# Query projection of an attention branch as seven half-size products over pairs of token blocks, placed between the first products of a spectral branch

## The chip, the cores and the metric

One core of one Trainium2 chip. The metric is the device time of one execution in microseconds (us). TensorE (PE) multiplies, its weight loads are shown as PEld; VectorE (DVE), ScalarE (ACT) and GpSimd (POOL) work on tiles; SyncE (SP) issues the DMAs.

## The reference

Two independent branches write the two halves of each output row. x is 2048 x 1024 in both, all in float32.

```
# attention with 32 query heads of width 32 and one shared key/value head
q = (x @ wq) in 32 heads;  k = x @ wk;  v = x @ wv          # wq 1024x1024, wk and wv 1024x32
p = softmax(q k^T * 32**-0.5);  a = concat_heads(p v) @ wo  # wo 1024x1024
# spectral branch: real part of a 2-D Fourier transform by given matrices
re = xb @ dft_hid_re.T;  im = xb @ dft_hid_im.T
b = dft_seq_re @ re - dft_seq_im @ im
return concatenate([a, b], -1)
```

## The kernel before

**Products.** A float32 product is made of three matmuls of rounded parts (`hi` times `hi`, `hi` times `lo`, `lo` times `hi`). A `Group` is one 128x512 output in one PSUM bank: its `left` items are weights (128 x 4 x 128 each), its `right` items 128x512 operands, and it has three matmuls for each right operand. One such matmul is a *fill*; `pos["fill"]` counts them. The query projection has 4 token blocks x 8 groups of 128 output columns, each with 8 right operands (24 fills). Keys and values have one group of 24 fills for each block. The spectral branch is two stages of seven half-size products each (a Winograd form of Strassen's method): `STAGE1` with 16 groups of 12 fills for each product p1, p2, p6, p7, p5, p3, p4 in that order, then `PRODUCTS` with groups of 24. Last comes the output projection with groups of 24.

**Attention.** 32 units, one for each token block b and query group g, with 32 steps each. A step makes the scores twice on TensorE: `scores` (tile `pss`) for row maxima on VectorE (`nm`) and row sums on ScalarE, and for an earlier unit `expo` (tile `pst`), transposed, whose exponential on ScalarE is the tile `p`. Every eighth step `pv` multiplies four chunks of `p` with the values. `open_unit` fetches a unit's query (`qh_d`, `ql_d`) from DRAM and needs its stores to have been issued.

**Order.** All groups stand in one list. `take(n)` issues the next n fills; `level` spreads all fills evenly over the 1024 steps and gives none to the step that has a `pv`. The prologue (up to 494 fills) first runs START = 120 fills alone, then 66, then 7 with each of 44 steps that have scores only. `aside` moves a `pv` out of the first and last 6 fills of a group.

**Operands.** `pump` runs after each fill and moves two lines of items forward, `RL` for right operands and `ML` for left ones, each in four stages: load (SyncE), `comb` (sums of up to three terms on GpSimd, in place in `it.t[0]`), `hi` (a rounding cast, ScalarE up to START, then VectorE) and `lo` (the difference, VectorE up to START, then GpSimd). The two lines are

```
RL = Line(NR0, NR, (40, 40, 14, 8), load_r, comb, hi_r, lo)
ML = Line(NM0, NM, (52, 36, 27, 21), load_m, comb, hi_m, lo)
```

with the lead of each stage in fills before an item's due time. `may` lets at most NR0 = NM0 = 3 items be between load and `lo`. A left item is due when its group needs it. The right operands of a new set are due spread over the set before:

```
p0 = prev["set"]
it.due = min(it.need, p0 + (i0 - p0) * (g.first + c + 1) // (len(g.set) * len(g.right)))
```

Every engine and SyncE's queue keep the order in which the program issues.

**Outputs.** `post` of a group moves its PSUM bank to SBUF. For the query it writes `qh` (scaled and rounded) and `ql` (the rest), both on VectorE after START, and stores them. For the spectral stage it copies, or adds to a partial output that was loaded again (`ys`, tile `y`). `store` issues a DMA at once up to START and 9 fills later (`BEHIND`) after that.

The rounded weights of the query are saved in DRAM by block 0 (`wq_d`) and fetched by the other three. The order of the list is: keys and values of blocks 1, 2, 3, 0, the query of blocks 0, 1, 2, 3, the spectral stages, the output projection.

Of the kernel before, what the change touches and what calls it, by code (L numbers as in the profile page):

```python
# [8 lines left out]
F32 = mybir.dt.float32  # L9
F32R = mybir.dt.float32r  # L10
AF = mybir.ActivationFunctionType
ALU = mybir.AluOpType
# [4 lines left out]
P = 128  # L17
# [4 lines left out]
W = 512  # L22
NG = 8
NQ = 4
# [22 lines left out]
STAGE1 = [  # L47
# [7 lines left out]
]  # L55
# [32 lines left out]
def tile_kernel(ctx: ExitStack, tc, xT, wq, wkv, wo, xbT, wT, cT, out):  # L88
    nc = tc.nc
    te = Ordered(tc, nc.tensor)  # L90
    act = Ordered(tc, nc.scalar)
    dve = Ordered(tc, nc.vector)
    gp = Ordered(tc, nc.gpsimd)
    sp = Ordered(tc, nc.sync)
    scale = float(DH) ** -0.5
# [5 lines left out]
    dram = ctx.enter_context(tc.tile_pool(name="dram", bufs=1, space=DRAM))  # L101
# [5 lines left out]
    wq_d = [[[dram.tile([P, 4, P], F32, name=f"wq_{g}_{q}_{a}") for a in range(2)] for q in range(2)] for g in range(NG)]  # L107
# [283 lines left out]
    def x_set(b):  # L391
        return [Item([(lambda c=c: xT[b, c], 1)]) for c in range(ND)]
# [23 lines left out]
    def kv_group(b, xs):  # L416
        return Group(wkv_items, xs, kv_post(b), rows=2 * DH)

    ready = set()
    seen_w = set()  # L420

    def q_group(b, g, xs):
        if g in seen_w:
            left = [Item(None, pre=lambda q=q: wq_d[g][q]) for q in range(2)]
        else:
            seen_w.add(g)
            left = [Item([(lambda q=q: wq[g, :, q * 4:(q + 1) * 4, :], 1)], save=wq_d[g][q]) for q in range(2)]

        def post(ps):
            qh = op.tile([P, W], F32R, name="qh")  # L430
            ql = op.tile([P, W], F32R, name="ql", bufs=1)
            if pos["fill"] <= START:
                act.activation(qh, ps, AF.Copy, scale=scale)
            else:
                dve.tensor_scalar_mul(qh, ps, scale)
            dve.scalar_tensor_tensor(ql, ps, scale, qh.bitcast(F32), op0=ALU.mult, op1=ALU.subtract)
            store(qh_d[b][g], qh)
            store(ql_d[b][g], ql, ("q", b, g))
        return Group(left, xs, post)


    s_d = {(r, e): [dram.tile([P, W], F32, name=f"s{r}{e}_{s}") for s in range(NC)] for r in range(2) for e in range(2)}
    COLS = (((0, 0), (1, 1)), ((1, 0), (0, 1)))

    def stage1():
        for f, (name, lt, rt, outs) in enumerate(STAGE1):
            keeps = any(t[0] == name for p in STAGE1 for t in p[1] + p[2])

            def x_src(t, k):
                if isinstance(t[0], str):  # L450
                    return (lambda: have(("xr", k), xr_d[k]), t[1])
                return (lambda: xbT[t[0] * 8 + k, :, t[1] * 4:t[1] * 4 + 4], t[2])

            def w_src(t, n, c):
                if isinstance(t[0], str):
                    return (lambda: have(("wr", n, c), wr_d[n][c]), t[1])
                r, e = COLS[n][t[0]]
                return (lambda: wT[r, e, t[1] * 4 + c], t[2])

            R = [[Item([w_src(t, n, c) for t in rt], raw=(wr_d[n][c], ("wr", n, c)) if keeps else None) for c in range(4)]  # L460
                 for n in range(2)]
            for k in range(8):
                left = [Item([x_src(t, k) for t in lt], raw=(xr_d[k], ("xr", k)) if keeps else None)]
                for n in range(2):
                    ys, plan = [], []
                    for frm, sg, to in outs:
                        it = None
                        if frm is not None:
                            it = Item([(lambda frm=frm, n=n, k=k: have((n, frm, k), u_d[n, frm][k]), 1)])
                            ys.append(it)  # L470
                        if isinstance(to, str):
                            plan.append((it, sg, u_d[n, to][k], (n, to, k)))
                        else:
                            me, s = COLS[n][to[1]], to[0] * 8 + k
                            plan.append((it, sg, s_d[me][s], (me, s)))

                    def post(ps, plan=plan):
                        for it, sg, to, key in plan:
                            if it is None:
                                o = op.tile([P, W], F32, name="qh")  # L480
                                dve.tensor_copy(o, ps)
                            else:
                                o = it.y
                                (dve.tensor_add if sg > 0 else dve.tensor_sub)(o, o, ps)
                            store(to, o, key)
                    yield Group(left, R[n], post, ys=ys, part=(R, 4 * n))

    hs = {}

    def have(key, ap):  # L490
        assert key in ready, key
        return ap

    def stage2():
        seen, total = {}, {}
# [67 lines left out]

    def x_groups(b, kv, q):
        xs = x_set(b)
        return ([kv_group(b, xs)] if kv else []) + ([q_group(b, g, xs) for g in range(NG)] if q else [])

    first = x_groups(0, True, True)  # L570
    start = x_groups(1, True, False) + x_groups(2, True, False) + x_groups(3, True, False) + first[:2]
# [263 lines left out]
```

## Time and profile before

| | |
|---|---|
| time, median of 3 runs | 2852.16 us (2851.02 to 2853.55) |
| span of the profiled execution, first to last instruction | 2849.5 us |
| product matmuls by the plan | 5664, of which the query projection has 768 |
| mean granted clock of TensorE | 0.998 |
| DMA | 480.83 MB, mean 169 GB/s |

The page gives the span of the profiled execution and not its own time; the median lies 2.7 us above the span. The page's busy shares count the modelled end of each matmul, and matmuls overlap, so the sum of the durations of a group of matmuls is more than the time they take. The fills pass at about 164 us the end of the prologue (494 fills); the spectral stage begins at fill 864.

### The profile page before, as it was taken

The numbers are of one execution on the slowest core, as the hardware profiler recorded it, in microseconds if no ns is written. First come the engines' busy times: TensorE is split into PE (matmuls) and PEld (weight loads), VectorE is DVE, ScalarE is ACT, GpSimd is POOL, SyncE is SP. The second block draws the span as 40 slices with busy tenths as digits, with TensorE's granted clock in tenths as the row PEclk, the third lists the DMA queues.
The fourth block names the chain that finished last, engine by engine and source line by source line (L and its number), as shares of the span: only waits on it lengthen the run. The fifth ranks groups of instructions, "written<-read, shape, count | busy, mean of one in ns | idle before, by whom it ended". The sixth has DMA issues, their size and how long they took to land.

```text
span 2849.5 us, 39944 instructions
## 1 busy us (share of the span) xinstructions
PE 2793.9 (98%) x13904; PEld 1927.6 (68%) x13904; DVE 1941.3 (68%) x2430; ACT 2188.4 (77%) x3151; POOL 1212.0 (43%) x928
## 2 busy tenths in 40 slices
PE   8999999999999999999999999999999999999999
PEld 5777666767666676766666667667667676667656
DVE  6776676767777677767776776777777776756511
ACT  4578887878878888878788888778878787888740
POOL 1211123454423336555664454785766653520000
PEclk9999999999999999999999999999999999999999
DMA  8865425665576455454452454564554533554445
GB/s 292 291 196 176 150 97 166 230 222 186 188 236 205 166 182 160 148 163 130 160 186 96 126 162 127 178 204 141 176 169 149 179 120 99 163 152 137 126 141 170
DMA packets 315722, 480.83 MB, mean 169 GB/s; under 512 B 33408, under 2 KB 98432, under 8 KB 315520
## 3 DMA queue, kind: packets, MB, share of 16 engines
q1 hardware_dynamic: 315520, 478.28, 52.6%
q8 instruction: 109, 1.79, 0.3%
q14 instruction: 93, 0.76, 0.1%
HBM read 364.12 MB, written 112.98 MB: 167 GB/s over the span
## 4 chain that ended last, share of the span: by engine, by line
PE 85%; DVE 5%; ACT 3%; issue 2%; DMA 2%; POOL 1%; SPq 1%; POOLq 0%; ACTq 0%; DVEq 0%
PE psb L66 54%; PE pst L66 16%; PE pss L66 15%; ACT p L66 2%; DVE nm L66 2%; ACT pss L66 1%; DVE mh L66 1%; SPq L66 1%; DVE rh L66 1%; DVE ov L66 1%; POOL m L66 1%; DMA r<-s 1%; POOL ml L66 0%; DMA r<-in_xT_dram 0%; DMA m<-in_wq_dram 0%
## 5 line engine op out<-in xcount | busy, mean ns | idle before, releaser
L66 DVE TENSOR_REDUCE nm<-pss 128x1 f32<-128x1024 f32 x1024 | 1248.2, 1221 | 396.0 <-PE pss L66 394.0
L66 ACT ACTIVATE p<-pst 128x1024 f32<-128x1024 f32 x1024 | 1051.3, 1027 | 431.2 <-PE pst L66 424.5
L66 ACT ACTIVATE pss<-pss,nm 128x1024 f32<-128x1024 f32 x1024 | 1113.5, 1087 | 146.1 <-DVE nm L66 136.8
L66 PE MATMUL psb<-rh,mh 128*128 128x512 f32 (+1 forms) x1852 | 730.7, 395 | 11.3 <-ACT rh L66 8.3
L66 PE MATMUL psb<-rh,ml 128*128 128x512 f32 (+1 forms) x1852 | 730.2, 394 | 0.7 <-POOL ml L66 0.7
L66 PE MATMUL psb<-rl,mh 128*128 128x512 f32 (+1 forms) x1852 | 729.4, 394 | 0.3 <-DVE rl L66 0.3
L66 PE MATMUL pst<-qst,kst 128*128 128x512 f32 x2048 | 659.8, 403 | 20.7 <-ACT p L66 20.0
L66 PE MATMUL pss<-kst,qst 128*128 128x512 f32 x2048 | 657.8, 402 | 10.0 <-ACT pss L66 9.8
L66 POOL TENSOR_TENSOR ml<-m,mh 128x512 fp32r<-128x512 f32 x292 | 383.3, 1313 | 506.6 <-DVE mh L66 290.6
L66 POOL TENSOR_TENSOR rl<-r,rh 128x512 fp32r<-128x512 f32 x214 | 280.5, 1311 | 741.8 <-DVE rh L66 562.5
L66 PEld LDWEIGHTS pss<-kst,qst 128*128 128x128 f32 x2048 | 374.0, 188 | 198.5 <-issue 93.0
L66 PEld LDWEIGHTS pst<-qst,kst 128*128 128x128 f32 x2048 | 370.5, 188 | 151.5 <-ACT p L66 71.9
L66 PE MATMUL psb<-p,v 128*32 128x512 f32 x4096 | 466.0, 595 | 1.6 <-DVE y L66 1.4
L66 PEld LDWEIGHTS psb<-rh,mh 128*128 128x128 f32 (+1 forms) x1852 | 347.4, 188 | 96.8 <-ACT rh L66 9.4
L66 PEld LDWEIGHTS psb<-rl,mh 128*128 128x128 f32 (+1 forms) x1852 | 347.2, 187 | 84.8 <-DVE rl L66 1.4
L66 PEld LDWEIGHTS psb<-rh,ml 128*128 128x128 f32 (+1 forms) x1852 | 347.1, 187 | 84.5 <-POOL ml L66 1.1
L66 PEld LDWEIGHTS psb<-p,v 128*32 128x32 f32 x4096 | 120.0, 109 | 277.6 <-issue 259.0
L66 POOL TENSOR_TENSOR m<-m,m 128x512 f32<-128x512 f32 x192 | 254.6, 1326 | 7.1 <-DMA m<-in_cT_dram 5.6
L66 DVE TENSOR_TENSOR ov<-ov,psb 128x512 f32<-128x512 f32 x96 | 65.9, 687 | 263.9 <-PE psb L66 263.8
L66 POOL TENSOR_TENSOR r<-r,r 128x512 f32<-128x512 f32 x112 | 148.3, 1325 | 200.5 <-DMA r<-in_wT_dram 99.9
L66 ACT ACTIVATION_READ_ACCUMULATOR pss<-pss,nm 128x1 f32 x1024 | 208.6, 204 | 0.0
L66 DVE CAST mh<-m 128x512 fp32r<-128x512 f32 x291 | 171.2, 588 | 18.3 <-POOL m L66 9.8
(68 smaller groups left out, 835.8 us busy)
## 6 DMA issues: line engine op xcount, KB each, us to landing
m<-in_cT_dram SPq DMA_DIRECT2D x384, 256.0 KB, 3.7
r<-s SPq DMA_DIRECT2D x192, 256.0 KB, 4.3
y<-y SPq DMA_DIRECT2D x96, 256.0 KB, 4.5
r<-in_wT_dram SPq DMA_DIRECT2D x80, 256.0 KB, 4.1
m<-in_xbT_dram SPq DMA_DIRECT2D x80, 256.0 KB, 3.9
y<-u SPq DMA_DIRECT2D x80, 256.0 KB, 2.9
qst<-qh SPq DMA_DIRECT2D x64, 256.0 KB, 5.5
s<-y SPq DMA_DIRECT2D x64, 256.0 KB, 3.2
```

The lines of the kernel that those rows point to most:

```text
L66: return lambda *a, **k: self.tc.keep_in_program_order(f(*a, **k))
```

## The change

Two token blocks (a pair, 1024 tokens) and the two halves of the query's 1024 output columns and of the 1024 inputs make a 2x2 by 2x2 block product. It is computed with the seven products of `STAGE1`, each with 4 groups (128 columns each) of 4 right operands, 12 fills. Sums of weights and of token operands are made by the items' `comb`; partial outputs t, u2, u3 and u4 go to DRAM and come back as `ys`. The stage-1 generator becomes a function `winograd` that both use, with a scale for the query.

The final output of a query group is cast to `qh` on VectorE and its rest `ql` is made on GpSimd after START. Pair 0 saves the rounded (summed) weights of each product, pair 1 fetches them. p1 and p2 of pair 0 use the operands of block 0 that the key/value group has made; p1's output stays in SBUF for p2 and is stored as well. The list's order becomes: keys and values 1, 2, 3, 0; query p1 and p2 of pair 0, alternating; spectral p1; query p6 of pair 0; spectral p2; query p7 and p5 of pair 0; p1 of pair 1; p3 and p4 of pair 0; p2, p6, p7, p5, p3, p4 of pair 1; spectral p6, p7, p5, p3, p4; the second spectral stage and the output projection as they were.

```
-    def q_group(b, g, xs):
...
-            dve.scalar_tensor_tensor(ql, ps, scale, qh.bitcast(F32), op0=ALU.mult, op1=ALU.subtract)
...
+    def winograd(tag, products, nm, ns, litem, rsrc, rraw, mid, last, scale=None):
+
+        for name, lt, rt, outs in products:
...
+            R = [[Item([src(t, n, c) for t in rt], raw=(rraw[n][c], (tag, "r", n, c)) if keeps else None) for c in range(4)]
+                 for n in range(ns)]
+            for k in range(nm):
+                left = [litem(name, lt, k)]
+                for n in range(ns):
...
+                    def post(ps, plan=plan, n=n, k=k):
+                        for it, sg, to in plan:
                             if it is None:
                                 o = op.tile([P, W], F32, name="qh")
...
+                                    dve.tensor_scalar_mul(o, ps, scale)
                             else:
                                 o = it.y
...
+                                    dve.scalar_tensor_tensor(o, ps, sg * scale, o, op0=ALU.mult, op1=ALU.add)
+                            if isinstance(to, str):
+                                store(mid[n, to][k], o, (tag, n, to, k))
+                            else:
+                                last(to, n, k, o)
                     yield Group(left, R[n], post, ys=ys, part=(R, 4 * n))
...
+    def q_item(p, name, lt, k):
+        if p:
+            return Item(None, pre=lambda: wq_d[name, k])
...
+            return (lambda: wq[t[0] * 4 + k, :, t[1] * 4:t[1] * 4 + 4, :], t[2])
...
+    def q_out(p):
+        def last(to, n, k, o):
+            b, g = 2 * p + to[1], to[0] * 4 + k
+            qh = op.tile([P, W], F32R, name="qh")
+            ql = op.tile([P, W], F32R, name="ql", bufs=1)
+            cast(qh, o)
+            (dve if pos["fill"] <= START else gp).tensor_sub(ql, o, qh.bitcast(F32))
+            store(qh_d[b][g], qh)
+            store(ql_d[b][g], ql, ("q", b, g))
+        return last
...
+    def q_products(p, names):
+        return list(winograd(("q", p), [x for x in STAGE1 if x[0] in names], 4, 1, lambda *a: q_item(p, *a),
+                             lambda t, n, c: xT[2 * p + t[0], t[1] * 4 + c], [xq_d[p]], uq_d[p], q_out(p), scale))
+
+    def q_first(xs):
...
+            gs.append(Group([q_item(0, "p1", [(0, 0, 1)], k)], xs[:4], post1, part=([xs], 0)))
+            gs.append(Group([q_item(0, "p2", [(0, 1, 1)], k)], xs[4:], post2, part=([xs], 4)))
...
-    START = 24 * len(start)
-    rest = first[2:] + x_groups(1, False, True) + x_groups(2, False, True) + x_groups(3, False, True)
-    rest += list(stage1()) + list(stage2())
+    start = [kv_group(b, xs[b]) for b in (1, 2, 3, 0)] + first[:2]
+    START = sum(3 * len(g.right) for g in start)
+    rest = first[2:]
+    rest += stage1(["p1"]) + q_products(0, ["p6"]) + stage1(["p2"]) + q_products(0, ["p7", "p5"])
+    rest += q_products(1, ["p1"]) + q_products(0, ["p3", "p4"])
+    rest += q_products(1, ["p2", "p6", "p7", "p5", "p3", "p4"])
+    rest += stage1(["p6", "p7", "p5", "p3", "p4"]) + list(stage2())
```

More of the change, by code (lines that the diff above doesn't have):

```diff
@@ L442, in tile_kernel, with have @@
[L442 to L449, printed above, removed]
-                if isinstance(t[0], str):
[L451 to L464, printed above, removed]
+    def have(key, ap):
+        assert key in ready, key
+        return ap
@@ L468, in stage1 @@
                         if frm is not None:
-                            it = Item([(lambda frm=frm, n=n, k=k: have((n, frm, k), u_d[n, frm][k]), 1)])
+                            it = Item([(lambda frm=frm, n=n, k=k: have((tag, n, frm, k), mid[n, frm][k]), 1)])
                             ys.append(it)
[L471 to L475, printed above, removed]
@@ new lines, in tile_kernel, with stage1, x_item, src @@
+    s_d = {(r, e): [dram.tile([P, W], F32, name=f"s{r}{e}_{s}") for s in range(NC)] for r in range(2) for e in range(2)}
+    COLS = (((0, 0), (1, 1)), ((1, 0), (0, 1)))
+    def stage1(names):
+        def x_item(name, lt, k):
+            def src(t):
+                if isinstance(t[0], str):
+                    return (lambda: have(("xr", k), xr_d[k]), t[1])
+                return (lambda: xbT[t[0] * 8 + k, :, t[1] * 4:t[1] * 4 + 4], t[2])
+            keeps = any(t[0] == name for p in STAGE1 for t in p[1])
+            return Item([src(t) for t in lt], raw=(xr_d[k], ("xr", k)) if keeps else None)
+        def w_src(t, n, c):
+            r, e = COLS[n][t[0]]
+            return wT[r, e, t[1] * 4 + c]
+        def last(to, n, k, o):
+            me, s = COLS[n][to[1]], to[0] * 8 + k
+            store(s_d[me][s], o, (me, s))
+        return list(winograd("s", [x for x in STAGE1 if x[0] in names], 8, 2, x_item, w_src, wr_d, u_d, last))
@@ L560, in o_group @@
         return Group([o_left(b, t, q) for q in range(2)], ws, post)
[L566 to L571, printed above, removed]
-    START = 24 * len(start)
-    rest = first[2:] + x_groups(1, False, True) + x_groups(2, False, True) + x_groups(3, False, True)
-    rest += list(stage1()) + list(stage2())
+    xs = [x_set(b) for b in range(NQ)]
+    first = q_first(xs[0])
+    start = [kv_group(b, xs[b]) for b in (1, 2, 3, 0)] + first[:2]
[5 more added lines that the diff above has]
+    rest += stage1(["p6", "p7", "p5", "p3", "p4"]) + list(stage2())
     w1, w0 = wo_set(1), wo_set(0)
```

58 lines of the change are left out of this document (33 added, 25 removed).

## The prediction

> **What bounds the kernel now.** I read the page first, then the chain of waits, then the groups of the stretch in which the query projection runs, and at last the waits and the order of time on GpSimd (POOL) there. The page:
>
> ```profile
> span 2849.5 us, 39944 instructions
> PE 2793.9 (98%) x13904; PEld 1927.6 (68%) x13904; DVE 1941.3 (68%) x2430; ACT 2188.4 (77%) x3151; POOL 1212.0 (43%) x928
> ...
> POOL 1211123454423336555664454785766653520000
> PEclk9999999999999999999999999999999999999999
> ...
> PE 85%; DVE 5%; ACT 3%; issue 2%; DMA 2%; POOL 1%; SPq 1%; POOLq 0%; ACTq 0%; DVEq 0%
> ```
>
> TensorE is busy 98% of the span and makes 85% of the chain that ended last, at an undisturbed clock. A matmul taken away is therefore worth its time, unless something else becomes late. POOL is at one to two tenths in the first slices (the query projection) and at five and more later. Most executions end 2.7 us above this span (2852.16 median against 2849.5), so I work with the span and add 2.7 at the end.
>
> What one matmul costs is best seen at the tail of the chain in order of time, and what a step costs in the prologue of the same view:
>
> ```profile
> 2823.75 21.92 PE psb L66 x96
> ...
> 88.58 0.46 PE pss L66 x2
> 89.04 1.62 PE psb L66 x7
> 90.67 0.46 PE pss L66 x2
> ```
>
> 96 product matmuls stand in a row for 21.92 us: 0.228 us each. In the prologue a step is two score matmuls and seven product matmuls, 2.09 us (90.67 less 88.58), 0.299 us a "fill" (one product matmul of the plan).
>
> Now the groups between 164 and 600 us, query projection and first spectral products, kept apart by shape:
>
> ```profile
> L66 PE MATMUL psb<-rh,mh 128*128 128x512 f32 x273 | 107.3, 393 | 0.0
> L66 PE MATMUL psb<-rh,ml 128*128 128x512 f32 x273 | 107.2, 393 | 0.0
> L66 PE MATMUL psb<-rl,mh 128*128 128x512 f32 x272 | 106.8, 393 | 0.0
> L66 POOL TENSOR_TENSOR rl<-r,rh 128x512 fp32r<-128x512 f32 x35 | 45.5, 1301 | 223.0 <-DVE rh L66 138.7 <-PE psb L66 54.5 <-issue 20.6
> L66 POOL TENSOR_TENSOR r<-r,r 128x512 f32<-128x512 f32 x12 | 15.5, 1295 | 34.7 <-DMA r<-in_wT_dram 29.6 <-issue 5.0
> L66 POOL MEMSET qst<- 32x2048 f32 x5 | 9.0, 1809 | 0.3
> L66 DVE CAST mh<-m 128x512 fp32r<-128x512 f32 x20 | 10.7, 535 | 0.0
> L66 DVE CAST rh<-r 128x512 fp32r<-128x512 f32 x34 | 15.0, 441 | 0.0
> ```
>
> 818 fills in 436 us: 0.533 us a fill, since the score, transposed-score and value matmuls run between them. A POOL pass over a 128x512 tile takes 1.30 us whatever it does.
>
> **Part 1, the products removed.** Before: 4 blocks x 8 groups x 24 = 768 fills. After: 2 pairs x 7 products x 4 groups x 12 = 672. 96 are gone, exactly the number in the tail row, so 21.9 us, if the steps stay bound by TensorE. Whether ScalarE then sets the step is seen in its order of time:
>
> ```profile
> 424.88 1.08 ACT L66 ACTIVATE pss<-pss,nm 128x1024 f32<-128x1024 f32 x1
> 425.88 0.20 ACT L66 ACTIVATION_READ_ACCUMULATOR pss<-pss,nm 128x1 f32 x1
> 426.05 1.03 ACT L66 ACTIVATE p<-pst 128x1024 f32<-128x1024 f32 x1
> 426.97 1.08 ACT L66 ACTIVATE pss<-pss,nm 128x1024 f32<-128x1024 f32 x1
> ```
>
> Its shortest step is 2.09 us (426.97 less 424.88), which is four score matmuls and five fills (9 x 0.232 by the prologue row). The plan spreads 4954 fills over 1024 steps, after the change 4858, and gives none to one step in eight: 5.53 a step, then 5.42. Both are above five, so the full 21.9 us stands; below five a fill would be worth nothing.
>
> **Part 2, where covers hold: nothing.** The prologue keeps its 494 fills, START stays 120, and the first attention unit waits for the same 24 product matmuls. VectorE gains 24 casts of right operands, 12 of left ones and 32 of the query: (24 + 32) x 0.44 + 12 x 0.54 = 31 us, its work on PSUM outputs keeps its count (64 passes). DMAs grow by some 176 of 256 KB (loads for sums, partial outputs out and in, weights saved, less 40 fetches). Both have room in the main stretch, and groups of 12 fills instead of 24 cost TensorE nothing visible:
>
> ```profile
> 164.00:465.00 301.00, 298.15 (x1496) 206.65 (x1496) 203.09 (x251) 247.97 (x358) 54.03 (x41) 1.00 0.46 148
> 465.00:560.00 95.00, 94.11 (x482) 63.46 (x481) 67.56 (x90) 76.62 (x113) 44.07 (x34) 1.00 0.61 204
> ```
>
> The columns are PE, PEld, DVE, ACT, POOL busy, granted clock, DMA share, GB/s. Groups of 24 (164 to about 360) and of 12 (465 to 560, with the sums of three-term operands on POOL) both leave TensorE at 99%. Its price is bounded by 0 and 1% of 310 us; I take 0.
>
> **Part 3, POOL, the cost I expect.** POOL runs its instructions in order. For a summed right operand `RL` has the same lead, 40 fills, for load and sum, so the sum stands behind its own load:
>
> ```profile
> 476.30 1.29 POOL L66 TENSOR_TENSOR ml<-m,mh 128x512 fp32r<-128x512 f32 x1 [7.24 <-DVE mh L66]
> 481.63 1.29 POOL L66 TENSOR_TENSOR r<-r,r 128x512 f32<-128x512 f32 x1 [4.03 <-DMA r<-in_wT_dram]
> 483.01 1.29 POOL L66 TENSOR_TENSOR r<-r,h 128x512 f32<-128x512 f32 x1
> 484.27 1.28 POOL L66 TENSOR_TENSOR rl<-r,rh 128x512 fp32r<-128x512 f32 x1
> ...
> POOL r L66 <- DMA r<-in_wT_dram: 29.6, 8, 5.4
> ```
>
> The last row is POOL's waits from 465 to 600 us: eight operands, eight waits, 3.7 us each. There the next set is spread over 192 fills (102 us), and an operand every 24 fills can afford it. After the change the set before is often only 48 fills long (25.6 us), and the load of operand j also needs the staging buffer that the low half of operand j-3 frees on POOL (NR0 is 3). Behind a waiting POOL are queued: the sums and low halves of the weights, `ql` of each finished query group, and the SyncE queue's loads into the same buffers. VectorE waits for it in turn, since its casts are in order with the row maxima that every score step needs.
>
> Three places:
> - *Spectral p6 behind query p4 of the second pair* (fills 1073 to 1173). Its eight three-term operands were prepared over 192 fills; their due times now fall into the 48 of one query product. POOL's work: 16 sums, 8 + 2 low halves, 7 `ql`, two left tiles of three passes, a memset: 39 x 1.30 + 1.8 = 52.5 us, against 100 x 0.533 = 53.3 us. It fits only if no load wait shows; eight of 3.7 us make 29.6. Bounds 0 and 29. With three staging buffers at six fills' distance most waits must show: I take 20.
> - *The other query products in the main stretch.* Over 48 fills (25.6 us) query p7 of pair 0 needs 4 x (1.3 + 3.7 + 1.3) for p5's right operands and 4 x 2.6 for weights, 35.6 us; p2 of pair 1 needs 4 x (2.6 + 3.7 + 1.3) for p6's and 5.2 for `ql`, 35.6 us. Each is 10 us over. Right operands may be late by 17 fills (9 us), the weights' casts only by 9 (4.8 us). Bounds 0 and 20; I take 8.
> - *Query p6 of pair 0, in the prologue* (48 x 0.299 = 14.3 us). POOL: 12 passes for weights, 8 low halves, the memset: 27.8 us, against 14.3 and the lead of 36 fills, 10.8. It is 2.7 us late, and one more load wait, 3.7, may stand ahead: bounds 0 and 10; I take 4.
>
> Sum: -21.9 + 20 + 8 + 4 = +10.1; span 2859.6, time 2862.3, **2862 us**. The own range of this case is POOL's delay of 24 to 45 us: 2854 to 2875.
>
> **The start could also move.** VectorE loses its wait for the `ql` buffer, POOL takes it. TensorE's stall there is this:
>
> ```profile
> 71.01 0.39 PE L66 MATMUL psb<-rh,ml 128*128 128x512 f32 x1
> 75.28 1.22 PE L66 MATMUL pss<-kst,qst 128*128 128x512 f32 x2 [3.88 <-ACT pss L66]
> 76.30 0.63 PE L66 MATMUL psb<-rh,mh 128*128 128x512 f32 x1
> 76.73 0.63 PE L66 MATMUL psb<-rl,mh 128*128 128x512 f32 x1
> ```
>
> It is worth 4 us at most, and partial outputs stored twice as often can bring as much: -4 to +4, I take 0. The rows show more: after the 3.88 us stall the matmuls start 0.43 us apart instead of 0.23.
>
> **Rivals.**
> *Covers hold (faster).* The leads absorb POOL's delay, as they did in the stretch 465 to 560, where POOL, busy 46% (44.07 of 95 us) and waiting 3.7 us for each operand, left TensorE at 99%. For it speaks that an average over the query products is not full: fills 588 to 1073 need 40 sums, 56 low halves, 24 `ql` and 3 memsets, 161 us, and 24 waits, 89 us: 250 of 485 x 0.533 = 258 us. Against it speak the peaks. With 0 to 16 us of delay the time is 2830 to 2846; at the middle, 8, it is 2838. It decides against my forecast once POOL's delay on TensorE is under 21.9 us.
> *Stalls with a half clock (much slower).* All load waits show (29 + 20 + 10 = 59 us), or each of some four stalls past 3.88 us is followed by some 12 matmuls 0.2 us longer, 2.4 us each, on top of the forecast. Time 2872 to 2889; taken 2878. What the change loses starts with the same queue, so it decides where POOL is late by over 45 us.
> By the Trainium skill, "TensorE: Matmul & The Clock Gate", "HAM oscillation", a TensorE idle for more than about 3.4 us falls back to half its clock; the trace agrees with its 3.88 us. By that rule this rival would follow from the stalls themselves, and the sum would be about 10 us above mine.
> *It doesn't do what it says:* a query group could miss its unit. The tightest is block 0, group 4: its product ends at fill 828, is stored at 837, and unit 4 opens at about fill 862 (494 + 4858 x 9.71 / 128): 25 fills, 13 us to spare. I give it no chance of its own.
>
> **How the numbers follow.** Forecast 0.52, covers hold 0.32, half clock and full waits 0.16. A measurement of this kernel can tell about 0.2% from no change, 5.7 us: 2846.5 to 2857.9 is "same". Nearly all of the second case is faster, 0.31; its remainder 0.01 and the lower end of the forecast, 0.10, are the same, 0.11; the rest, 0.42 + 0.16, is slower, 0.58. The range holds the second case whole and leaves out the upper end of the third (about 0.08) and, below, a start that gains on top of full covers: 2830 to 2886, some 0.15 outside.
>
> **What would show it.** Product matmuls 5568 instead of 5664; around 510 to 560 us POOL without idle time but its DMA waits, VectorE waiting for POOL's `r` and `m`, TensorE under 90% in a stretch of some 50 us, and a smaller dent near 130 us. From spectral p7 on nothing should differ but the 72 to 96 fewer fills. If TensorE stays at 99% there, Part 3 is wrong and the time is near 2832; if the dent lies elsewhere, the place is wrong.

## The result, and the profile after

The changed kernel takes 2986.10 us (median of 4 runs, 2979.02 to 2992.99); the ratio to the kernel before is 1.0476, 95% interval 1.0464 to 1.0488. It is slower, as forecast, but by 134 us instead of 10, and 100 us above the upper end of the forecast's range (2886). The profiled execution's span is 2985.9 us. The page of the changed kernel:

```profile
span 2985.9 us, 40193 instructions
PE 2823.4 (95%) x13808; PEld 1930.4 (65%) x13808; DVE 1994.6 (67%) x2499; ACT 2184.3 (73%) x3152; POOL 1374.2 (46%) x1054
PE   7899868759999999999999999999999999999999
...
POOL 2635444355333434655575346576666654420000
PEclk8999989879999999999999999999999999999999
...
PE 73%; DMA 8%; DVE 6%; POOL 4%; issue 4%; ACT 3%; SPq 2%; POOLq 0%; DVEq 0%; ACTq 0%
```

TensorE has 96 matmuls fewer, as the change says, and yet is busy 29 us longer; its granted clock falls in some of the first nine slices (75 us each). From the tenth on its busy share and its clock stand at nine tenths or more. The chain, 85% TensorE before, now has 8% DMA and 4% POOL.

To place the loss I use ScalarE's order of time. The *s*-th `ACTIVATE pss<-pss,nm` is the exponential of attention step *s*, and both kernels run the same 1024 of them. Two of them, steps 156 and 216, in the kernel before and then after:

```profile
450.17 1.08 ACT L66 ACTIVATE pss<-pss,nm 128x1024 f32<-128x1024 f32 x1
...
605.97 1.08 ACT L66 ACTIVATE pss<-pss,nm 128x1024 f32<-128x1024 f32 x1
```

```profile
529.42 1.09 ACT L66 ACTIVATE pss<-pss,nm 128x1024 f32<-128x1024 f32 x1
...
752.38 1.08 ACT L66 ACTIVATE pss<-pss,nm 128x1024 f32<-128x1024 f32 x1
```

The changed kernel is 79.3 us late at the one and 146.4 us at the other: 67.1 us are lost between them. Here is the lateness, in us against the kernel before, at the steps that bound the places of Part 3, with kernels that come below:

| step (kernel before, us) | 0 (67) | 24 (124) | 36 (150) | 72 (237) | 156 (450) | 216 (606) | 1023 (2693) |
|---|---|---|---|---|---|---|---|
| after | 6.3 | 1.3 | 15.6 | 15.4 | 79.3 | 146.4 | 134.9 |
| e1_out_buffers | 3.0 | -3.3 | 9.2 | 9.1 | 37.9 | 89.8 | 79.0 |
| e2_staging | 3.0 | -1.6 | 9.8 | 9.0 | 18.6 | 45.5 | 46.2 |
| e4_both | 0.0 | -5.6 | 5.6 | 5.1 | 12.1 | 39.4 | 42.7 |
| e3_order | 4.5 | -0.6 | 31.3 | 74.4 | 146.6 | 145.8 | 138.2 |
| e16_staging5_ring14 | 3.4 | -1.4 | 9.9 | 9.0 | 21.6 | 50.8 | 39.3 |

So the prologue's query product p6 of pair 0 costs 14.3 us (steps 24 to 36), the query products that follow 63.9 (72 to 156), spectral p6 behind the last of them 67.1 (156 to 216). Then nothing is lost any more, and 11.5 us come back.

The same by time, in the table by stage of the changed kernel (PE, PEld, DVE, ACT, POOL busy, granted clock, DMA share, GB/s):

```profile
308.00:470.00 162.00, 122.76 (x523) 79.06 (x522) 90.89 (x121) 86.79 (x126) 71.45 (x55) 0.88 0.64 208
552.00:685.00 133.00, 87.42 (x355) 53.69 (x355) 57.56 (x68) 55.69 (x80) 68.66 (x54) 0.81 0.67 224
800.00:900.00 100.00, 99.81 (x509) 69.10 (x508) 74.11 (x95) 82.85 (x120) 36.94 (x29) 1.00 0.58 191
```

In the two bad stretches TensorE is busy 76% and 66% at a granted clock of 0.88 and 0.81, while no other engine is busy more than 57% and the DMA share is under 0.7. On average nothing is full. Engines that are all partly idle wait for one another. The waits of the whole run of the changed kernel (us in total, times, longest) name the partners:

```profile
POOL r L66 <- DMA r<-in_wT_dram: 115.2, 29, 9.8
...
POOL r L66 <- DMA r<-in_xT_dram: 103.1, 30, 8.2
DVE qh L66 <- DMA qh<-qh: 74.6, 19, 8.1
POOL ql L66 <- DMA ql<-ql: 67.6, 20, 8.0
DVE mh L66 <- POOL m L66: 53.1, 19, 15.9
```

Two of these have no price in Part 3 of the prediction: `qh` and `ql` wait for the stores of the output that last held their buffer. One turn of the loop, in POOL's order of time and then in that of SyncE's queue:

```profile
404.34 1.26 POOL L66 TENSOR_TENSOR ql<-y,qh 128x512 fp32r<-128x512 f32 x1 [1.62 <-DMA ql<-ql]
405.56 1.26 POOL L66 TENSOR_TENSOR rl<-r,rh 128x512 fp32r<-128x512 f32 x1
410.39 1.28 POOL L66 TENSOR_TENSOR r<-r,r 128x512 f32<-128x512 f32 x1 [3.57 <-DMA r<-in_xT_dram]
413.23 1.26 POOL L66 TENSOR_TENSOR r<-r,h 128x512 f32<-128x512 f32 x1 [1.56 <-DMA h<-in_xT_dram]
415.82 1.26 POOL L66 TENSOR_TENSOR ql<-y,qh 128x512 fp32r<-128x512 f32 x1 [1.33 <-DMA ql<-ql]
417.04 1.26 POOL L66 TENSOR_TENSOR rl<-r,rh 128x512 fp32r<-128x512 f32 x1
```

```profile
406.85 0.81 SPq L66 DMA_DIRECT2D r<-in_xT_dram  x2
407.71 0.42 SPq L66 DMA_DIRECT2D h<-in_xT_dram  x1
408.23 0.38 SPq L66 DMA_DIRECT2D mh<-wq  x1
408.71 0.38 SPq L66 DMA_DIRECT2D ml<-wq  x1
409.17 0.38 SPq L66 DMA_DIRECT2D qh<-qh  x1
409.61 0.42 SPq L66 DMA_DIRECT2D ql<-ql  x1
...
418.32 0.81 SPq L66 DMA_DIRECT2D r<-in_xT_dram  x2
```

The low half `rl` ends at 406.82 and frees a staging buffer. SyncE had stood at the loads for that buffer and issues them at 406.85; behind them, in order, stood the fetches of weights and the stores of `qh` and `ql`. POOL waits 3.57 us for the load, makes the sum, waits for the store of the last `ql`, which went out at 409.61 behind that load, and only then comes to the next `rl` at 417.04, which releases the next load at 418.32. One operand in 11.5 us (417.04 less 405.56). The plan gives each 12 fills of 0.533 us, 6.4 us. POOL is at work for 5 of the 11.5 us. The turn shown is one of the longer ones: from 308 to 470 us there are 16 `rl`, 9.9 us apart in the mean. Without `ql` and the wait for its store (2.6 us) it would take 8.9 us, an estimate from its rows, and that is still above 6.4. Slower loads are not the reason: from issue to landing the loads `r<-in_wT_dram` take 3.0 us in the median from 552 to 685 us, against 4.1 us in the kernel before from 465 to 600 us. The stores of `ql` do land later, 5.4 us after issue (308 to 470 us) against 2.8 us before (316 to 450 us), and this lengthens the turn. The waits of SyncE's queue from 308 to 470 us say the same from the other side, 15 times 5.2 us:

```profile
SPq L66 <- POOL rl L66: 77.3, 15, 8.1
```

From there it goes to TensorE by way of VectorE, whose casts stand in order with the row maxima of the score steps. In the order of time of VectorE, then of TensorE, of the changed kernel:

```profile
632.08 1.47 DVE L66 CAST mh<-m 128x512 fp32r<-128x512 f32 x1 [15.87 <-POOL m L66]
```

```profile
622.11 0.39 PE L66 MATMUL psb<-rh,mh 128*128 128x512 f32 x1
636.37 1.22 PE L66 MATMUL pss<-kst,qst 128*128 128x512 f32 x2 [13.87 <-ACT pss L66]
...
638.30 0.63 PE L66 MATMUL psb<-rl,mh 128*128 128x512 f32 x1
638.73 0.63 PE L66 MATMUL psb<-rh,ml 128*128 128x512 f32 x1
```

VectorE stands 15.87 us at a left operand's cast. TensorE waits 13.87 us for the bank of its next scores, which ScalarE reads after VectorE's row maxima, and then works at half clock, 0.43 us from matmul to matmul.

### The profile page after: what moved, and what is told of

Same layout as the page of the kernel before. It is cut to its first block, busy times and chain, and to the rows that moved or that the text cites. A ratio compares the mean times of both kernels' runs of the same rounds, so it can differ in the third digit from the quotient of the medians.

```text
span 2985.9 us, 40193 instructions
## 1 busy us (share of the span) xinstructions
PE 2823.4 (95%) x13808; PEld 1930.4 (65%) x13808; DVE 1994.6 (67%) x2499; ACT 2184.3 (73%) x3152; POOL 1374.2 (46%) x1054
## 4 chain that ended last, share of the span: by engine, by line
PE 73%; DMA 8%; DVE 6%; POOL 4%; issue 4%; ACT 3%; SPq 2%; POOLq 0%; DVEq 0%; ACTq 0%
PE psb L66 46%; PE pst L66 14%; PE pss L66 13%; DVE nm L66 2%; ACT p L66 2%; DMA ql<-ql 2%; SPq L66 2%; DMA qh<-qh 1%; POOL rl L66 1%; POOL m L66 1%; ACT pss L66 1%; POOL ml L66 1%; DVE mh L66 1%; DMA r<-in_xT_dram 1%; DVE rh L66 1%
## 5 line engine op out<-in xcount | busy, mean ns | idle before, releaser
L66 PE MATMUL pss<-kst,qst 128*128 128x512 f32 x2048 | 666.0, 406 | 74.6 <-ACT pss L66 74.4
L66 PE MATMUL pst<-qst,kst 128*128 128x512 f32 x2048 | 670.3, 409 | 22.8 <-ACT p L66 21.9
L66 POOL TENSOR_TENSOR ml<-m,mh 128x512 fp32r<-128x512 f32 x304 | 399.3, 1314 | 460.0 <-DVE mh L66 202.0
L66 POOL TENSOR_TENSOR rl<-r,rh 128x512 fp32r<-128x512 f32 x237 | 312.1, 1317 | 495.9 <-DVE rh L66 397.6
L66 POOL TENSOR_TENSOR r<-r,r 128x512 f32<-128x512 f32 x144 | 189.7, 1318 | 337.8 <-DMA r<-in_wT_dram 115.2
L66 POOL TENSOR_TENSOR m<-m,m 128x512 f32<-128x512 f32 x208 | 276.3, 1328 | 11.6 <-DMA m<-in_cT_dram 7.8
L66 DVE CAST mh<-m 128x512 fp32r<-128x512 f32 x303 | 186.0, 614 | 59.9 <-POOL m L66 53.1
```

Of the source, the lines that this page charges most:

```text
L66: return lambda *a, **k: self.tc.keep_in_program_order(f(*a, **k))
```

## The experiments

Each ratio is to the kernel before, run beside it, with its 95% interval. Edits are to the changed kernel where nothing else is said.

**e1_out_buffers**: `ql` needs no buffer of its own and `qh` has three.

```
-    op = pool(ctx, "op", 2, side="right")
+    op = pool(ctx, "op", 3, side="right")
-            ql = op.tile([P, W], F32R, name="ql", bufs=1)
+            ql = o.bitcast(F32R)
```

> The query's low half is written in place over the tile of the sum it comes from (a ring of six) instead of into the one ql buffer, and there are three buffers for qh instead of two; nothing else changes. Theory A (the output buffers: POOL waited 67.6 us for ql's store and VectorE 74.6 us for qh's, and both queue up behind loads in SyncE's one queue): about 100 us faster than the changed kernel, 2880 to 2910, both rows gone. Theory B (the sums' staging loop: low half frees a buffer, the load follows, POOL waits for it): the two rows go, POOL's waits for in_xT and in_wT loads (218 us together) stay, 2950 to 2980. Theory C (eight three-term operands of spectral p6 in 48 fills): under 40 us of gain, the stretch of p6's operands (some 130 us for fills 1068 to 1188) stays.

Measured 2930.49 us, 1.0274 (1.0257 to 1.0292): 56 us less than the changed kernel, between what theory A and theory B expected. The waits for these stores are gone, those for loads are as in the changed kernel:

```profile
POOL r L66 <- DMA r<-in_wT_dram: 118.8, 30, 9.8
...
POOL r L66 <- DMA r<-in_xT_dram: 106.7, 31, 10.0
```

**e2_staging**: five staging buffers for the first terms of right operands instead of three, and with `NR0` four for second terms instead of two. The ring of finished right operands has 12 instead of 14.

```
-    NR0, NM0, NY = 3, 3, 6
-    NR, NM = 14, 4
+    NR0, NM0, NY = 5, 3, 6
+    NR, NM = 12, 4
```

> Five staging buffers for right operands instead of three; to make room the ring of finished right operands has 12 pairs instead of 14. Theory A: under 30 us faster, 2955 to 2986, the ql and qh waits stay. Theory B: 80 to 120 us faster, 2870 to 2910, POOL's waits for in_xT and in_wT loads fall from 218 us to under 80. Theory C: 20 to 40 us faster.

Measured 2897.56 us, 1.0167 (1.0152 to 1.0183): 89 us less, as theory B expected, though POOL's waits for the two loads fall only to 140 us and not under 80. From 300 to 450 us the `rl` stand 6.6 us apart in the mean (23 of them), the plan's pace. With the output buffers left alone, the waits for stores fall too, `ql` from 67.6 to 30.5 us and `qh` from 74.6 to 14.3:

```profile
POOL ql L66 <- DMA ql<-ql: 30.5, 15, 4.8
DVE qh L66 <- DMA qh<-qh: 14.3, 4, 7.6
```

**e4_both**: the edits of e1 and e2 together.

> e1 and e2 together. If A and B are two halves of one loop, each alone leaves the other and both together take nearly all: 2835 to 2865. If A alone is the cause this equals e1, if B alone it equals e2. If the order (theory C) is the cause, 2920 or more.

Measured 2896.52 us, 1.0162 (1.0146 to 1.0177). 56 and 89 us do not add: together they bring 90. The 2835 to 2865 us that two halves of a loop should have brought are missed, and the time equals e2's. So the staging buffers alone open the loop, and the waits for `ql` and `qh` are a part of its turn, not a second half beside it.

**e3_order**: spectral p2 is moved from between the query products to just before spectral p6, as a spacer.

```
-    rest += stage1(["p1"]) + q_products(0, ["p6"]) + stage1(["p2"]) + q_products(0, ["p7", "p5"])
+    rest += stage1(["p1"]) + q_products(0, ["p6", "p7", "p5"])
...
-    rest += stage1(["p6", "p7", "p5", "p3", "p4"]) + list(stage2())
+    rest += stage1(["p2", "p6", "p7", "p5", "p3", "p4"]) + list(stage2())
```

> Only the order: spectral p2 (192 fills, one-term operands) stands between the query's last product and spectral p6, instead of between query p6 and p7. The query's products then follow each other without a pause. Theory C: 60 to 75 us faster, 2910 to 2930, since spectral p6's operands get 192 fills again. Theories A and B: the loop between SyncE and POOL stays in the other query products, and with query p7's operands now due over 48 fills of the prologue it grows there: 2925 to 2975.

Measured 2987.37 us, 1.0482 (1.0466 to 1.0497), the same time as the changed kernel within the intervals, and above both cases of the expectation. The table of steps shows more than the time: nothing is lost at spectral p6 any more (steps 156 to 216: -0.8 us instead of 67.1), and all of it is lost earlier, 146.6 us by step 156. The 192 fills of p2 protect whatever stands behind them. Moving them moves the loss.

**e5_lead**: the sum is asked for 12 fills after its load, instead of at the same time.

```
-    RL = Line(NR0, NR, (40, 40, 14, 8), load_r, comb, hi_r, lo)
+    RL = Line(NR0, NR, (40, 28, 14, 8), load_r, comb, hi_r, lo)
```

> Of the changed kernel only RL's lead of the sum goes from 40 to 28 fills, so a right operand's load is issued 12 fills ahead of its sum. If the equal lead is what makes POOL wait (Part 3 of the prediction): POOL's waits for in_xT and in_wT (218 us) halve and the time falls by 50 or more, to below 2935. If the loop over three staging buffers is (low half, then load, then sum): the load can't go earlier than the low half of the operand three before, the waits stay within 20%, and the time stays at 2965 to 2995.

Measured 2971.66 us, 1.0430 (1.0414 to 1.0445). This attacks the very wait that Part 3 priced. It removes four fifths of it and brings 14 us. The time is the one expected of the loop, but the waits, which were to stay within 20% with it, fall much further. The waits of e5_lead:

```profile
POOL ql L66 <- DMA ql<-ql: 95.2, 17, 8.7
...
POOL r L66 <- DMA r<-in_wT_dram: 28.6, 10, 4.0
...
POOL r L66 <- DMA r<-in_xT_dram: 17.5, 8, 3.8
```

POOL's waits for these two loads go from 218.3 us (115.2 + 103.1) to 46.1, those for `ql`'s store from 67.6 to 95.2. From step 72 to step 216 the two load waits fall by 112 us, and POOL's whole idle time only from 264 to 250 us. In a closed loop a wait taken away at one station is mostly waited at the others. The rows of waits say where the loop stands still, not what it costs.

**e6_ql_dve**: `ql` is made by VectorE always, as in the kernel before.

```
-            (dve if pos["fill"] <= START else gp).tensor_sub(ql, o, qh.bitcast(F32))
+            dve.tensor_sub(ql, o, qh.bitcast(F32))
```

> Of the changed kernel only ql of the query goes from POOL back to VectorE. If the POOL queue's mixture matters (POOL waits for ql's store and holds up the low halves that free the staging buffers): 40 to 80 us faster, 2905 to 2945. If the single ql buffer blocks whichever engine writes it: VectorE, which serves every score step, now waits instead, within 20 us or slower, 2970 to 3010.

Measured 2936.95 us, 1.0312 (1.0295 to 1.0329): 49 us less, though the wait for the store did not go away. VectorE has it now:

```profile
POOL r L66 <- DMA r<-in_wT_dram: 129.2, 30, 10.0
...
POOL r L66 <- DMA r<-in_xT_dram: 101.8, 28, 8.4
DVE ql L66 <- DMA ql<-ql: 61.4, 16, 7.0
```

POOL's `rl` no longer stands behind that wait. Three different edits (a buffer, a staging buffer, an engine) take 49 to 89 us each out of the same 134.

**e8_fewer_fills**: the kernel *before*, without its four output groups of one token block and half, 96 fills.

```
-    rest += [o_group(b, t, e, ws) for e, ws in ((1, w1), (0, w0)) for b in range(NQ - 1) for t in range(4)]
+    rest += [o_group(b, t, e, ws) for e, ws in ((1, w1), (0, w0)) for b in range(NQ - 1) for t in range(4) if (e, b) != (1, 0)]
```

> The kernel before without the four output groups of token block 0, right half (4 x 24 = 96 fills; that part of the output is not computed), nothing else. What 96 fills are worth when no stall is added: 21.9 us by the prediction's price of 0.228 (2828 to 2832); if ScalarE sets part of the steps, as the slope of 11.5 us for 75.6 fills over steps 216 to 1023 of the changed kernel says, 12 to 16 us (2835 to 2841).

Measured 2832.25 us, 0.9941 (0.9927 to 0.9956), 16.8 us less by this ratio (12.5 to 20.8); by the spans 17.3 (2849.5 less 2832.2). That lies between the two cases expected: 0.18 us a fill, not 0.228. The changed kernel's own slope is near it: over the 807 steps from 216 on it has 96 x 807 / 1024 = 76 fills fewer and gains 11.5 us, 0.15 each. The removed matmuls are worth about 17 of the 21.9 us of Part 1.

**e7_spread** and **e9_raw_from_pool**: both on e4_both. e7 keeps right operands at least 10 fills apart in their due times; e9 in addition lets GpSimd's queue store the sums that are kept for later products.

```
+    for i in range(len(RL.items) - 1, 32, -1):
+        x, y = RL.items[i - 1], RL.items[i]
+        x.due = min(x.due, y.due - 10)
```

```
-            store(it.raw[0], it.t[0], it.raw[1])
+            move(gp, it.raw[0], it.t[0])
+            ready.add(it.raw[1])
```

> e4 (ql in place, three qh, five staging buffers, ring of 12) and the due times of right operands pulled ahead so that two of them are at least 10 fills apart. If what is left in e4 is the bunching of spectral p6's operands in 48 fills (27 us between steps 168 and 180 there): that dent goes and the time is 2862 to 2876. If POOL or the ring of 12 is the limit there: no gain, 2888 to 2900.

> e7 with one edit: the kept sums of p6 (four of the query's, eight of the spectral right operands, their left ones too) are stored by GpSimd's own queue right behind the sum, instead of by SyncE 9 fills later, where each store waits for its sum and the loads of the next operand stand behind it. If SyncE's order is what holds the next load there (one operand each 8.1 us in e7's trace between 494 and 542 us): the operands come every 5 to 6 us and the dent of 22.6 us between steps 168 and 180 shrinks under 10: 2872 to 2884. If POOL's own passes are the limit: 2888 to 2900, or slower by the issue time on POOL.

Measured 2894.48 us, 1.0157 (1.0140 to 1.0174), and 2891.58 us, 1.0133 (1.0116 to 1.0150). Neither differs clearly from e4_both, and both lie in the second case expected, a limit in POOL's own passes (or, for e7, the ring of 12). The loss between steps 156 and 216 is 27.3 us in e4_both, 24.2 in e7 and 17.5 in e9, but at step 216 all three are 37.4 to 39.4 us late: what e9 saves at spectral p6 it loses before.

**e10_staging4_ring14** and **e16_staging5_ring14** ask what the two ring buffers given up in e2 cost. Both write `ql` in place with two `qh` and 14 ring buffers. e10 has four staging buffers for first terms and two for second ones; e16 has five and two, and one `y` tile less. In e16:

```
-    NR0, NM0, NY = 3, 3, 6
+    NR0, NM0, NY = 5, 3, 5
...
-                return i < min(self.n[3] + self.nstage, self.n[1] + self.nstage - 1)
+                return i < min(self.n[3] + self.nstage, self.n[1] + 2)
...
-                it.t.append(r0p.tile([P, W], F32, name=f"r{n}", bufs=NR0 - n))
+                it.t.append(r0p.tile([P, W], F32, name=f"r{n}", bufs=(NR0, 2)[n]))
```

> The changed kernel with ql in place (two qh), four staging buffers for first terms, two for second ones as before, and the full ring of 14. If the buffers that a low half frees are the loop: between e1 and e4 for the stall (30 to 55 us left by step 216), and without the 10 us that e2 and e4 lose after step 496 if the ring of 12 makes those: 2885 to 2910. If only the second-term buffers count: like e1, 2920 to 2935.

> The order of the changed kernel with e13's buffers (ring of 14). If e4's loss after step 496 is the ring of 12: as e4 up to step 216 (about 40 us late), and 10 us better at the end, 2880 to 2890. If two buffers for second terms make the loop again: 2900 to 2925.

Measured 2906.88 us, 1.0193 (1.0177 to 1.0208), and 2893.18 us, 1.0144 (1.0120 to 1.0167). e10 lies in its first case: with one more buffer for first terms it is 24 us under e1, which points to the buffers that a low half frees. e16 lies between its two cases. Between steps 496 and 736, in the second spectral stage, the kernels with a ring of 12 lose 11.1 us (e2) and 12.8 us (e4), those with 14 lose 1.2 (e10) and 1.7 us (e16). So e2's ring costs some 11 us far from the change; e16 keeps the ring, but is 50.8 us late at step 216 against 39.4 for e4.

**e11_new_order**, **e12_new_order_staging5**, **e13_light_before** put other products in front of spectral p6. e11 is e10 and e12 is e4_both, both in a new order; e13 has e16's buffers and an order of its own:

```
e11, e12:
+    rest += stage1(["p1", "p6"]) + q_products(0, ["p6", "p7", "p4"]) + stage1(["p2", "p7", "p5"])
+    rest += q_products(0, ["p5", "p3"]) + q_products(1, ["p1", "p2", "p6", "p7", "p5", "p3", "p4"])
+    rest += stage1(["p3", "p4"]) + list(stage2())
e13:
+    rest += stage1(["p1", "p2"]) + q_products(0, ["p6", "p7", "p4"]) + q_products(0, ["p5", "p3"])
+    rest += q_products(1, ["p1", "p2"]) + stage1(["p6", "p7", "p5"])
+    rest += q_products(1, ["p6", "p7", "p5", "p3", "p4"]) + stage1(["p3", "p4"]) + list(stage2())
```

> e10 with another order: spectral p1, p6; query p6, p7, p4 of pair 0; spectral p2, p7, p5; query p5, p3 of pair 0 and all of pair 1; spectral p3, p4. No set of eight two- or three-term operands follows a query product, and query p6 of pair 0 is out of the prologue. If bunching in 48 fills is what is left beside the loop: 10 to 25 us above 2833 by step 216, 2845 to 2865, near the kernel before. If query products in a row stall by themselves (their own 4 operands in 48 fills): 2870 to 2900.

> e4 (five staging buffers, ring of 12, three qh) in the order of e11. Bunching: 2850 to 2870, of which 10 for the ring of 12. Query products in a row: 2870 to 2895.

> ql in place, two qh, five staging buffers for first terms and two for second ones, the full ring of 14, five y tiles instead of six. Order: spectral p1, p2; query p6, p7, p4, p5, p3 of pair 0; p1, p2 of pair 1 (one-term operands, fetched weights); spectral p6, p7, p5; the rest of pair 1; spectral p3, p4; stage 2. So no summed set is made in the prologue, and spectral p6 follows light query products. Bunching: the prologue's 11 us are gone, the dent at spectral p6 shrinks from 27 to 5 to 15, five query products with weights to sum in a row cost 10 to 15: 2850 to 2870. If any eight three-term operands in 48 fills cost 25 or more whatever stands before: 2870 to 2890.

Measured 2896.16 us, 1.0157 (1.0141 to 1.0172); 2902.63 us, 1.0179 (1.0164 to 1.0194); 2901.64 us, 1.0175 (1.0160 to 1.0191). e12 and e13 lie above both of their cases; e11's time lies in that of query products in a row, but most of its loss is elsewhere: it is 26.6 us late at step 44, the end of the prologue, where spectral p6 now begins, and its query products (steps 213 to 304) add some 15 us. In e13 the operands of spectral p6 are prepared at steps 120 to 132, and 26.3 us are lost there, though two query products of pair 1, without sums of weights, stand before it; in e16 it costs 29.2 us at its old place (steps 156 to 216). With the staging buffers of e2, e4, e13 and e16, spectral p6 behind a short product costs 26 to 29 us at both places.

**e14_light_spread** and **e15_light_spread_dve**: e13 with due times 10 fills apart (e7's edit), then also `ql` on VectorE (e6's edit).

> e13 with the due times pulled ahead to at least 10 fills between two operands, so spectral p6's eight reach back over both light query products. Bunching: 5 to 15 us below e13, 2840 to 2860. POOL's or SyncE's own pace: within 5 us of e13.

> e14 with ql on VectorE. If POOL's passes are what is left: another 5 to 10 us below e14. If not: within 3 us, or a few us slower by VectorE's added 28 passes of 0.7 us.

Measured 2904.52 us, 1.0187 (1.0171 to 1.0202), and 2903.04 us, 1.0182 (1.0167 to 1.0198): nothing. So neither the bunching of due times nor the `ql` passes on POOL make the rest. Sums and low halves stay on POOL in both, so POOL's own pace is not excluded; it is the second case expected of e14.

**e17_left_lead** and **e18_all_leads**: both on e16. There VectorE still waits for a left operand's sum inside spectral p6, as its order of time shows:

```profile
551.30 1.47 DVE L66 CAST mh<-m 128x512 fp32r<-128x512 f32 x1 [13.42 <-POOL m L66]
```

e17 asks for left loads and sums 12 fills earlier; e18 also for right loads 16 and right sums 4 fills earlier, with due times 10 fills apart.

```
-    ML = Line(NM0, NM, (52, 36, 27, 21), load_m, comb, hi_m, lo)
+    ML = Line(NM0, NM, (64, 48, 27, 21), load_m, comb, hi_m, lo)
e18 also:
-    RL = Line(NR0, NR, (40, 40, 14, 8), load_r, comb, hi_r, lo)
+    RL = Line(NR0, NR, (56, 44, 14, 8), load_r, comb, hi_r, lo)
```

> e16 with ML's leads of load and sum at 64 and 48 fills instead of 52 and 36; cast and low half as they were. If VectorE's 13.4 us before the cast of the left sum is the dent's second half: it goes, the dent falls from 30 to 15 to 20 us, 2876 to 2884. If GpSimd's total pace in these 48 fills sets the dent, the wait moves to a right operand: 2888 to 2896.

> e17, and RL's leads of load and sum at 56 and 44 instead of 40 and 40, and due times at least 10 fills apart. If leads cure it: 2855 to 2875. If GpSimd's total pace sets it: 2885 to 2897.

Measured 3174.61 us, 1.1132 (1.1113 to 1.1150), and 2979.86 us, 1.0455 (1.0435 to 1.0475). All four cases expected were far too low. e17 is 63.2 us late at step 216 (e16: 50.8) and 327.3 at the last step: 264 us are lost mostly in the second spectral stage, where the changed kernel loses nothing. Its waits:

```profile
POOL r L66 <- DMA r<-s: 434.4, 72, 8.2
POOL m L66 <- DMA m<-in_cT_dram: 280.5, 93, 5.6
DVE mh L66 <- POOL m L66: 261.5, 95, 6.9
```

In e16 the middle row was

```profile
POOL m L66 <- DMA m<-in_cT_dram: 7.8, 9, 1.5
```

With three staging buffers a left load can't be issued before the low half of the item three before it, whatever its lead says. That low half has kept its lead of 21 fills, and left items are 12 fills apart, so the load could move to 57 fills ahead at most, 5 earlier, while the sum moved by 12. POOL now waits 3 us each time, and SyncE's queue waits 1307 us for `ml` in all instead of 837 in e16: it looks like a second loop of the same kind, with left operands. That it is this loop alone is not shown. e18 has still more of the middle wait (435.3 us) but almost none of the first (0.5 us), and is late by 126.2 us at the last step instead of 327.3, so right and left operands act together. Up to step 216 e18 gains: it is 37.0 us late there, 13.8 less than e16, and spectral p6 costs 20.1 us.

None of the versions beats the kernel before; the nearest of those that compute all of it, e9, is 1.3% above it.

## Why the prediction was wrong: a delay that feeds itself

**Part 1** was over-priced a little: 17 us for 96 fills instead of 21.9. The rate of the tail row, 0.228 us, holds where product matmuls stand alone; inside the steps a fill brought 0.18. What takes the other 5 us is not shown. The 2.7 us added to the span are a little much as well: the profiled run of the changed kernel took 2987.69 us with a span of 2985.9, 1.8 us more.

**Part 2** failed in one item. That "groups of 12 fills instead of 24 cost TensorE nothing visible" was read from the spectral stage, whose outputs go through the six `y` tiles. The query's final outputs go through one `ql` and two `qh` buffers, are made every 12 fills in some products, and are stored 9 fills later at the end of SyncE's queue. The count of passes was right and the life of the buffers was not looked at. The output buffers (e1) are worth 56 us alone and 1 us beside e2's (e4), the engine of `ql` (e6) 49 us alone.

**Part 3** is where most was lost. It named the engine, the direction and the three places, and each price was too small. Predicted 4 us (0 to 10) in the prologue, 8 (0 to 20) for the other query products, 20 (0 to 29) for spectral p6; measured 14.3, 63.9 and 67.1. All three lie above their upper bounds. The failed step is the bound itself: passes of 1.30 us plus one load wait of 3.7 us each, with all waits showing, was taken for the worst. That counts POOL as a server with a fixed price for each operand. The 3.7 us came from a stretch of the kernel before (465 to 600 us) in which SyncE's queue never waits for POOL's `rl`. Where a load is issued only when POOL has freed the buffer, and the store that POOL waits for stands in the same queue behind that load, price and queue depend on each other: 9.9 us a turn in the mean, 11.5 in the turn shown, against 6.4 us planned. The sentence that held this, "the load of operand j also needs the staging buffer that the low half of operand j-3 frees on POOL", stands in the prediction, and was not carried into the sum. That e1 and e2 together bring no more than e2, that e2 brings the turn down to 6.6 us, and that e5 takes away 172 us of waits for 14 us of time, shows the loop. With it opened, in e4, the three places cost 11.2, 7.0 and 27.3 us, near the prediction's bounds. So the passes and single waits were priced about right; the feedback was left out.

**The rival of the half clock** came true on top, but its own price, 2872 to 2889 us, is 97 us short too. Over TensorE's whole order of time I counted the gaps of more than 1.5 us between matmuls, 3 before (7.8 us in all), 27 after (100.0 us) and 11 in e4 (45.8 us), and the product matmuls of the fills that show 0.63 us, as at 638.30, instead of 0.39: 28 before, 112 after, 37 in e4. So some 92 us of the loss are longer stalls, and 84 x 0.2 = 17 us are fills at half clock, an estimate that leaves out the score matmuls between them, and gaps under 1.5 us are in neither. The rule of the Trainium skill that the prediction cited, "TensorE: Matmul & The Clock Gate", "HAM oscillation", that a longer idle time costs half the clock, agrees with the row at 636.37; its limit of about 3.4 us does not hold here (last section). It was a term of the sum, not a case beside it.

**The start** is 6.3 us late at step 0 and 1.3 us at step 24, by then inside -4 to +4. **The signs to look for** were the right ones: the dent, TensorE far under 90%, VectorE waiting for POOL's `r` and `m`, the smaller dent in the prologue, and nothing after spectral p7 but fewer fills. What I had not listed is that the middle, from 308 to 470 us, is as bad as spectral p6.

**What stays open.** Of the 134 us, 90 go when the loop is opened (e4). Of the 43 to 46 us that remain in e4, some 11 are the smaller ring in the second stage (e2 and e4 against e10 and e16), and 27 are lost at spectral p6: eight operands of three terms each in the 48 fills of one short product. Spacing of due times and fewer POOL passes did not remove it. Kept sums stored by another queue took 7 us off there (e9 against e7) and earlier loads and sums 9 (e18 against e16), and both lost it elsewhere. Why the rest stands is not settled. Two suspects stand in e4's trace: from 520 to 550 us POOL is busy 24 of 30 us while TensorE is busy 10, and the DMA share is 0.91, more than in the stretches shown above. No run takes sums off POOL or bytes off the DMA there. Stores on a DMA queue of their own were tried for the kept sums alone, not for `qh` and `ql`.

## What to carry to other kernels

Before pricing a finer division of work, follow each small buffer round: who frees it, in which queue the refill stands, what stands behind that in the same queue, and who waits for it. If the round comes back to its start, its time of turn is a rate, and the rate has to be compared with the plan's (here 9.9 us in the mean against 6.4), not the waits added up one by one. And a wait that shrinks in the waits view is worth something only if the turn gets shorter: e5 removed four fifths of POOL's waits for loads and a tenth of the loss.

## What the runs showed of the hardware

A stall of 13.87 us left TensorE at half clock, which was expected. Shorter ones can do it too. In TensorE's order of time in e16_staging5_ring14:

```profile
526.75 1.22 PE L66 MATMUL pss<-kst,qst 128*128 128x512 f32 x2 [7.47 <-ACT pss L66]
...
535.27 0.39 PE L66 MATMUL psb<-rh,mh 128*128 128x512 f32 x1
535.50 0.39 PE L66 MATMUL psb<-rl,mh 128*128 128x512 f32 x1
537.50 0.73 PE L66 MATMUL pss<-kst,qst 128*128 128x512 f32 x2 [1.62 <-ACT pss L66]
...
539.58 0.63 PE L66 MATMUL psb<-rh,mh 128*128 128x512 f32 x1
540.01 0.63 PE L66 MATMUL psb<-rl,mh 128*128 128x512 f32 x1
```

After 7.47 us of idle time the clock is back by 535.27, with 0.23 us from start to start. A gap of 1.62 us follows, and the starts are 0.43 us apart again. The 3.88 us on which the prediction based its rival is no lower limit.

Nor is there a sharp one. I took all gaps between matmuls after 100 us, in all twenty traces, that follow three product matmuls at full clock, and counted those with two or more product matmuls of 0.60 to 0.66 us among the next six. Of 124 gaps of 1 to 1.5 us 7 have them, of 43 of 1.5 to 2 us 16, of 64 of 2 to 2.5 us 48, of 55 of 2.5 to 3.5 us 44, and of 68 longer ones 64. It need not be two gaps close together: in e16 a gap of 2.31 us at 1705.04, with no other over 1 us for 100 us on either side, is followed by starts 0.43 us apart, and one of 2.84 us at 1895.23 by starts 0.23 us apart. What decides between them these traces do not show.
